# Two routed expert layers behind an attention: layer one's weights prepared in pieces of 1024 and 768 columns instead of 512 and 384

## The chip, the core and the metric

The kernel is written in Bass with the Tile framework and runs on one NeuronCore of one Trainium2 chip. The metric is device time in microseconds; a lower number is better. Five engines work side by side, each through its own instructions in a fixed order: TensorE (PE, with the weight load PEld), VectorE (DVE), ScalarE (ACT), GpSimd (POOL) and SyncE (SP). SP issues most of the transfers, POOL those that gather and scatter rows.

## The reference, cut to what matters

The input x has 7168 tokens of 192 numbers. An attention over the seven last tokens comes first, then a routed layer with eight experts and two experts per token, then a second one with one expert per token. The weights of a layer are the same size: per expert 192x1024 and 1024x192.

```python
x = attn_out.reshape(B * S, D)                       # weighted sum over the 7 last tokens
# layer one
noisy = x @ w_gate + np.log1p(np.exp(x @ w_noise)) * noise
top2 = np.argpartition(-noisy, 2, axis=1)[:, :2]     # two experts of eight
h = np.maximum(x[mask] @ w1[e], 0.0)
out[mask] += top2_w[mask, k, None] * (h @ w2[e])
# layer two
logits = xn @ en.T / tau                             # normalised rows
expert_idx = np.argmax(logits, axis=1)
h = np.maximum(x[mask] @ w1[e], 0.0)
out[mask] = gate_w[mask, None] * (h @ w2[e])
```

## The kernel before

**Tiles.** The 7168 tokens stand as 56 columns of 128. Layer one handles them in three groups of columns, 0 to 24, 24 to 40 and 40 to 56. For a group the attention is computed in chunks of four columns, each chunk's rows are written to a table in DRAM (`t`, line 490) and its router products go to `lg`. When all chunks of a group are there, `ctl` chooses the experts (line 511 on ACT is the first step of that, line 514 the first on DVE), ranks the entries (577 to 593), lays out slots (605 on), makes lists of row numbers by products of one-hots (767 to 770 on DVE, 760 on PE), and decodes them into `gx` (795). From then on 256-row tiles of one expert can run: POOL gathers rows (978), PE transposes them (1006), ACT copies them (1008), `first_product` (1028, with 1030 on ACT and 1031 on DVE) and `second_product` (1054, 1059) run by turns for neighbouring tiles, and POOL scatters the results (1062).

**Head and body.** The head runs until the first group's lists are decoded. It holds the attention of 24 columns (six chunks of seven products on DVE, line 385, summed by PE, line 412), their rows, the routing, and the preparation of layer one's weights. The body is the tiles of both layers with everything else beside them.

**Preparation.** The products run in 16-bit floats, so `prep_gen` scales each weight matrix by a power of two, cuts it into a high and a low half and writes both into a table in DRAM (`ws`). It takes two experts at a time and has two jobs for each pair, m = 0 for w1 (three `wo` tiles of 2048 columns out) and m = 1 for w2 (two of 3072). A job loads 32-bit weights into a stage (line 276 to 281; for layer one the stages are the two weight buffers `wb` and the end of `xh`), squares them on ACT for the sums (294), adds over partitions on PE (305 to 309), makes the scale `wsc` on DVE (311, 238 to 240), and then splits piece by piece: ACT writes the high half as scaled copy (334), DVE subtracts it from the scaled weight for the low half (336). A finished `wo` tile (there are three buffers) goes out on SP (340 to 346). The pieces are 512 columns of w1 and two rows of 192, that is 384, of w2. Before a tile can run, SP loads its expert's weights from `ws` into `wb` (line 996), which needs all writes of `ws`.

**What sets the order.** In the head, `prep_gen` is a chain that takes one step at every point, a step ending at each `yield`. Every job has a rank, a priority that counts up with its instructions; routing starts from 0, attention and preparation both from 2000, the loads of group two from 18000. The scheduler of the framework then orders each engine's instructions by readiness in its own model and by that priority. So fewer instructions in a job also move what stands around them. Each engine carries out its instructions strictly in the order that comes out. SP issues loads in order too, and a step that waits (line 490 waits for a chunk's rows) holds up everything behind it.

Of the kernel before, what the change touches and what calls it, by code (L numbers as in the profile page):

```python
# [39 lines left out]
class Layer:  # L40
    """Static plan of one routed layer: k entries per token, column groups of tokens."""

    def __init__(self, k, groups, mixed):
        self.k, self.groups = k, groups
        self.np = N * k // 256
        self.cap = [b * 128 * k // 256 for _, b in groups]
        self.sec = [0] + [cdiv(b * 128 * k - E * 255, 256) for _, b in groups[:-1]]
        # mixed: the slot by which the entries of all groups but the last have been run
        self.done = [(groups[-2][1] * 128 * k + E * 255) // 256] if mixed else []
        # Each run of slots is taken from its start and from its middle by turns, one weight buffer for either,  # L50
        # so that a buffer is loaded anew only where its own half passes on to another expert.
        cuts = self.sec + self.done + [self.np]
        self.buf, self.fresh, order = {}, [], []
        for a, b in zip(cuts, cuts[1:]):
            m = a + cdiv(b - a, 2)
            self.fresh += [a, m]
            u = 0
            for j in range(b - a):
                s = (a, m)[j % 2] + j // 2
                self.buf[s] = len(self.buf) % 2  # L60
                order.append(("p", s))
                # the single units follow the first pairs that hold entries of every group
                left = NS - j
                if a == self.sec[-1] and 0 < left <= NS:
                    order.append(("s", u))
                    u += 1
        assert len(order) == self.np + NS
        self.order = order
        self.pos = {o: i for i, o in enumerate(order)}
        self.first = [self.pos[("p", s)] for s in self.sec]  # L70
        self.units = 2 * self.np + NS
# [3 lines left out]
def two_moe(ctx: ExitStack, tc: tile.TileContext, x, wgen, w_gate, w_noise, noise, w1a, w2a, emb, tau, w1b, w2b, out):  # L75
# [12 lines left out]
    work = ctx.enter_context(tc.tile_pool(name="work", bufs=2))  # L88
    psum = ctx.enter_context(tc.tile_pool(name="psum", bufs=1, space=bass.MemoryType.PSUM))
    V, A, PE, SP, PL = nc.vector, nc.scalar, nc.tensor, nc.sync, nc.gpsimd  # L90
# [59 lines left out]
    # masks by partition: all, below 64, from 64 on  # L150
# [9 lines left out]
    # an entry's value: (1 + partition / 128) 2^(place - 56)  # L160
# [94 lines left out]
    @contextmanager  # L255
    def urgent(l):
        """work of a patient job that would wait for ever on an engine that is never idle."""
        low = tc.cur_priority
        if l:
            tc.cur_priority = state["here"]  # L260
        yield
        if l:
            state["here"] = tc.cur_priority
            tc.cur_priority = low

    def prep_gen(l, w1, w2):
# [21 lines left out]
        for i, (e, m) in enumerate(jobs):  # L288
# [32 lines left out]
            for c in range(3 if m == 0 else 2):  # L321
                wo = prep.tile([128, 3072], F16, name="wo", bufs=3)
                if m == 0:
                    n = 2048
                    w = 512
                    pieces = [(wo[:, f:f + w], wo[:, 1024 + f:1024 + f + w], st[:, 1024 * c + f:1024 * c + f + w]) for f in range(0, 1024, w)]
                else:
                    n = 3072
                    wv = wo.rearrange("p (g a d) -> p g a d", a=2, d=D)
                    sv = st[:, 1536 * c:1536 * c + 1536].rearrange("p (g d) -> p g d", d=D)  # L330
                    w = 2
                    pieces = [(wv[:, g:g + w, 0], wv[:, g:g + w, 1], sv[:, g:g + w]) for g in range(0, 8, w)]
# [40 lines left out]
    def after_tile():  # L373
        """work beside a tile that stays behind the tile's own work that was issued before."""
        return tc.issue_after(state["pin"].ins) if "pin" in state else ExitStack()

    def after_product():
        """TensorE's work beside the tiles, which stays behind the products that were issued before."""
        return tc.issue_after(state["pe"].ins) if "pe" in state else ExitStack()
# [116 lines left out]
    def top1(v, m, dst, n):  # L496
        """dst: one-hot of the first largest of v; m: the largest."""
# [130 lines left out]
    def add_phase(l, lo, hi, at=None):  # L628
        """the pairs lo .. hi of every expert get the slots from `at` on, or those behind the phase before."""
# [24 lines left out]
    def slot_experts(l, s0, s1):  # L654
        """the experts of pair slots s0..s1 (float)."""
        yield from threshold(l, iof[:, s0:s1], s1 - s0, exec_e[l][:, s0:s1])
# [20 lines left out]
    def exec_tables(l, a, b):  # L677
        """integer tables of the slots a..b: the expert, and whether the weights have to be loaded."""
# [25 lines left out]
    def rows_of(dst, r, t, sh, phases, l, n):  # L704
        """rows of the ranks r of every expert, in the given phases."""
# [21 lines left out]
    def list_gen(l, L, g, row, n, nu, u0):  # L727
        """the entries of group g by row: onehots of a row's unit and place, multiplied."""
# [57 lines left out]
    def decode(l, v, n, us):  # L786
        """v: integers as floats, 128 (place + 71) + partition, or 0."""
# [20 lines left out]
    def left_over(l, L, g, lrow, fb, u0, nu):  # L808
        """adds the units that the section before g kept: full pairs in their place, and the rest, at the rows lrow."""
# [20 lines left out]
    def section_open(l, L, g, key):  # L830
        """full pairs of the tokens so far run; the rest of each expert is kept behind the last slot."""
# [48 lines left out]
    def left_ranks(l, g):  # L880
        """the ranks at which the two units begin that section g keeps of every expert."""
# [6 lines left out]
    def section_last(l, L, key):  # L888
# [11 lines left out]
        if L.done:  # L900
            # the pairs that end the entries of the groups before stand first
# [64 lines left out]
    def run_by(b):  # L966
        """the tile of layer one by which all entries of the tokens below column b have been run."""
        return L1.pos[("p", L1.done[0])] if b <= G1[-2][1] else base2
# [14 lines left out]
    def slot(i):  # L983
        """a tile's place in the tables of its layer, and the weights it uses."""
# [3 lines left out]
    def weights(i, part):  # L988
        """part 0: the first product's weights, part 1: the second's."""
# [23 lines left out]
    def first_product(i, bg):  # L1013
        """in four parts, taken by turns with those of the second product of the tile before."""
# [137 lines left out]
    class Job:  # L1152
        """A generator of work with its key, the tile it may start after, and its place in the order of issue."""
# [15 lines left out]
    class Queue:  # L1169
        """Work beside the tiles: chains go one step a point, threads as far as their share of VectorE goes."""  # L1170
# [164 lines left out]
```

## Time and profile before

| | |
|---|---|
| time, median of 3 runs | 1094.52 us (1091.99 to 1097.86) |
| span of the profiled execution | 1096.0 us (no time of its own beside the span is given; it lies inside the range of the runs) |
| PE busy | 946.8 us, 86% of the span |
| DVE busy | 700.7 us, 64% |
| ACT busy | 605.3 us, 55% |
| POOL busy | 407.3 us, 37% |
| gx of the first group written | 137.2 us from the start |
| first product of the first tile | 148.7 us from the start |

The span is the time from the first to the last instruction of one execution. Busy shares are averages over stages with different limits: PE is busy nearly all the time after 150 us and hardly at all between 87 and 148 us, where DVE and ACT work. So the head has to be read by its own rows, in order of time, and the body by PE's waits. A row of the timeline gives the start, the duration, the engine, the line and the tiles, and in brackets how long the engine was idle before and what ended that.

### The profile page before, as it was taken

The numbers are of one execution on the slowest core, as the hardware profiler recorded it, in microseconds if no ns is written. First come the engines' busy times: TensorE is split into PE (matmuls) and PEld (weight loads), VectorE is DVE, ScalarE is ACT, GpSimd is POOL, SyncE is SP. The second block draws the span as 40 slices with busy tenths as digits, with TensorE's granted clock in tenths as the row PEclk, the third lists the DMA queues.
The fourth block names the chain that finished last, engine by engine and source line by source line (L and its number), as shares of the span: only waits on it lengthen the run. The fifth ranks groups of instructions, "written<-read, shape, count | busy, mean of one in ns | idle before, by whom it ended". The sixth has DMA issues, their size and how long they took to land.

```text
span 1096.0 us, 27746 instructions
## 1 busy us (share of the span) xinstructions
PE 946.8 (86%) x10250; PEld 853.9 (78%) x10250; DVE 700.7 (64%) x1943; ACT 605.3 (55%) x1337; POOL 407.3 (37%) x384
## 2 busy tenths in 40 slices
PE   5891259899989999998989998988788999999996
PEld 2551248788878888998979897877678899999896
DVE  8996969889688979553434433988676733333331
ACT  2999336666465765555555543975265344444442
POOL 1000054443445454344334443333344444445422
PEclk9996569999999999999899999999899999999999
DMA  8789674556568564779798977866675736888751
GB/s 269 216 271 293 224 249 143 149 190 200 158 207 285 167 208 142 260 215 329 263 367 292 333 270 229 264 216 180 205 252 160 256 125 217 288 300 306 260 190 41
DMA packets 99464, 251.81 MB, mean 230 GB/s; under 512 B 14207, under 2 KB 65119, under 8 KB 89856
## 3 DMA queue, kind: packets, MB, share of 16 engines
q1 hardware_dynamic: 81664, 215.03, 57.9%
q0 software_dynamic: 17664, 35.01, 11.5%
q8 instruction: 80, 1.31, 0.5%
q14 instruction: 56, 0.46, 0.1%
HBM read 246.09 MB, written 58.69 MB: 278 GB/s over the span
## 4 chain that ended last, share of the span: by engine, by line
PE 32%; DMA 5%; issue 5%; DVE 3%; ACT 3%; POOL 3%; SPq 1%; another core or an unknown queue 1%; POOLq 0%; ACTq 0%
PE ph L1028 15%; PE py L1054 14%; DMA wb<-ws 3%; DMA xh<-ws 2%; PE pt L1006 1%; POOL xg L978 1%; PE bt L468 1%; POOL yb L1062 1%; ACT hh L1030 1%; POOL ss L536 1%; SPq L281 1%; ACT xt L473 1%; ACT xh L448 1%; PE bl L479 1%
## 5 line engine op out<-in xcount | busy, mean ns | idle before, releaser
L1028 PE MATMUL ph<-xt,wb 128*128 128x256 f16 x3360 | 422.6, 276 | 10.0 <-DVE hl L1031 4.1
L1054 PE MATMUL py<-wb,hh 128*128 128x192 f16 x2688 | 361.9, 248 | 17.9 <-ACT ys L1059 13.4
L1030 ACT ACTIVATE hh<-ph 128x512 f16<-128x512 f32 (+1 forms) x400 | 221.4, 560 | 269.7 <-PE ph L1028 209.7
L1028 PEld LDWEIGHTS <-wb 128*128 128x128 f16 x3360 | 327.3, 99 | 47.9 <-issue 9.7
L978 POOL DMA_INDIRECT xg<-t,gx x184 | 196.3, 1067 | 376.0 <-PE pt L1006 157.9
L1054 PEld LDWEIGHTS <-hh 128*128 128x128 f16 x2944 | 266.6, 99 | 28.0 <-issue 18.7
L1031 DVE SCALAR_TENSOR_TENSOR wt<-ph,hh 128x512 f16<-128x512 f32 x200 | 137.4, 689 | 116.6 <-ACT hh L1030 95.2
L1062 POOL DMA_INDIRECT yb<-ys,sx x120 | 131.5, 1096 | 198.0 <-ACT ys L1059 173.9
L1054 PE MATMUL py<-wb,wt 128*128 128x192 f16 x800 | 198.3, 248 | 0.2 <-issue 0.2
L1031 DVE SCALAR_TENSOR_TENSOR hl<-ph,hh 128x512 f16<-128x512 f32 (+1 forms) x200 | 118.9, 603 | 111.2 <-ACT hh L1030 87.6
L1054 PE MATMUL py<-wb,hl 128*128 128x192 f16 x544 | 134.9, 248 | 0.1
L1059 ACT ACTIVATE ys<-py,sc 128x192 f32<-128x192 f32 x184 | 68.0, 415 | 90.1 <-PE py L1054 74.3
L1062 POOL DMA_INDIRECT out_dram<-ys,sx x64 | 64.5, 1007 | 95.6 <-ACT ys L1059 83.5
L385 DVE TENSOR_TENSOR tmp<-xh,wt 128x768 f32<-128x768 f32 x90 | 84.9, 954 | 0.8 <-PE ph L412 0.7
L1054 PEld LDWEIGHTS <-wt 128*128 128x128 f16 x800 | 78.9, 99 | 0.8 <-issue 0.6
L1008 ACT ACTIVATE xt<-pt 128x768 f16<-128x768 f16 x84 | 67.7, 807 | 7.0 <-PE pt L1006 6.9
L1039 DVE TENSOR_SCALAR sc<-xg,csl 128x2 f32<-128x2 f32 (+1 forms) x100 | 23.0, 231 | 75.8 <-ACT ys L1059 60.2
L1054 PEld LDWEIGHTS <-hl 128*128 128x128 f16 x672 | 66.6, 99 | 0.2
L473 ACT ACTIVATE xt<-bt 128x768 f16<-128x768 f16 x56 | 45.2, 807 | 31.8 <-PE bt L468 21.9
L1006 PE MATMUL pt<-identh,xg 128*128 128x128 f16 x552 | 48.7, 222 | 11.6 <-DMA xg<-t,gx 11.4
L1028 PE MATMUL ph<-xt,xh 128*128 128x128 f16 x640 | 45.9, 223 | 7.4 <-DMA xh<-ws 4.7
L1006 PEld LDWEIGHTS <-xg 128*128 128x128 f16 x552 | 39.1, 99 | 14.4 <-DMA xg<-t,gx 11.9
(302 smaller groups left out, 1079.0 us busy)
## 6 DMA issues: line engine op xcount, KB each, us to landing
wb<-ws SPq DMA_DIRECT2D x84, 1024.0 KB
wb<-ws SPq DMA_DIRECT2D x84, 768.0 KB
xh<-ws SPq DMA_DIRECT2D x16, 1024.0 KB
ws<-wo SPq DMA_DIRECT2D x16, 768.0 KB
xh<-ws SPq DMA_DIRECT2D x16, 768.0 KB
tmp<-yb SPq DMA_DIRECT2D x28, 384.0 KB
ws<-wo SPq DMA_DIRECT2D x16, 512.0 KB
ws<-wo SPq DMA_DIRECT2D x32, 256.0 KB
```

Of the source, the lines that this page charges most:

```text
L385: V.tensor_mul(dst.rearrange("p t (h g) -> p (t h) g", g=G), xv, w)
L473: A.activation(xt.rearrange("p a n -> p (a n)"), pa[:, 0:768], AF.Copy)
L978: PL.indirect_dma_start(out=xg[:, h], out_offset=None, in_=T[l][0:rows_in], in_offset=bass.IndirectOffsetOnAxis(ap=gidx[l][:, u + h:u + h ...
L1006: PE.transpose(pt[:, j, h], xg[:, h, 128 * b:128 * b + 128], identh)
L1008: A.activation(xt.rearrange("p j h n -> p (j h n)"), pt.rearrange("p j h n -> p (j h n)"), AF.Copy)
L1028: state["pe"] = mark = PE.matmul(ph[:, q, :n], s, m, start=j == 0, stop=j == 4)
L1030: A.activation(hh[:, fs, :n], ph[:, :, :n], AF.Relu)
L1031: state["pin"] = V.scalar_tensor_tensor(hl[:, fs, :n], ph[:, :, :n], 0.0, hh[:, fs, :n], op0=ALU.max, op1=ALU.subtract)
L1039: V.tensor_scalar(sc[:, :nh], xg[:, :nh, 192:193].bitcast(F32).rearrange("p h o -> p (h o)"), csl[l][:, c:c + 1], None, op0=ALU.mult)
L1054: state["pe"] = PE.matmul(py[:, h], t[:, f, hs], w2[:, f, c], start=f == 0 and j == 0, stop=f == 7 and j == 2)
L1059: A.activation(ys[:, h], py[:, h], AF.Copy, scale=sc[:, h:h + 1])
L1062: d = PL.indirect_dma_start(out=dst, out_offset=bass.IndirectOffsetOnAxis(ap=sidx[l][:, u + h:u + h + 1], axis=0), in_=ys[:, h], in_offset ...
```

## The change

In `prep_gen` the width of a piece depends on the layer. For layer one (l = 0) a piece of w1 has 1024 columns instead of 512 and one of w2 four rows of 192 (768) instead of two (384). Layer two keeps its pieces. The remaining lines of the diff take out comments.

```diff
@@ -322,13 +322,13 @@
                 wo = prep.tile([128, 3072], F16, name="wo", bufs=3)
                 if m == 0:
                     n = 2048
-                    w = 512
+                    w = 512 if l else 1024
                     pieces = [...]
                 else:
                     n = 3072
                     wv = wo.rearrange("p (g a d) -> p g a d", a=2, d=D)
                     sv = st[:, 1536 * c:1536 * c + 1536].rearrange("p (g d) -> p g d", d=D)
-                    w = 2
+                    w = 2 if l else 4
                     pieces = [...]
                 for h, lo, v in pieces:
                     A.activation(h, v, AF.Copy, scale=sc[:, c:c + 1])
                     yield 0.1
                     V.scalar_tensor_tensor(lo, v, sc[:, c:c + 1], h, op0=ALU.mult, op1=ALU.subtract)
                     yield 0.6
```

Layer one has four pairs of experts, and a pair had 6 pieces of w1 and 8 of w2. So 56 pieces, each one ACT and one DVE instruction, become 28. The order on the engines changes with it at three places.

ACT in the middle of the head, at the fourth chunk of the attention (its router row sums are line 430, its scaling 437, its copy 439). Before:

```order
L430 ACTIVATE rows,nrm<-ph 128x192 x4
L294 ACTIVATE junk,wnr<-wb_131 128x1024
L437 ACTIVATE xs<-ph,sx 128x192 x4
L334 ACTIVATE wo<-wb_130,wsc 128x2x192
L439 ACTIVATE rows<-xs 128x4x192
```

and now:

```order
L430 ACTIVATE rows,nrm<-ph 128x192 x4
L334 ACTIVATE wo<-wb_131,wsc 128x1024
L437 ACTIVATE xs<-ph,sx 128x192 x4
L294 ACTIVATE junk,wnr<-xh 128x768
L439 ACTIVATE rows<-xs 128x4x192
```

The preparation is one job further on: a split piece (334), which needs its job's scale `wsc`, stands where a square (294) stood, ahead of the chunk's scaling.

ACT at the end of the head, from the last chunk's scaling to the first step of the choice of experts (511). Before:

```order
L437 ACTIVATE xs<-ph,sx 128x192 x4
L334 ACTIVATE wo<-wb_131,wsc 128x512
L439 ACTIVATE rows<-xs 128x4x192
L334 ACTIVATE wo<-wb_131,wsc 128x512
L294 ACTIVATE junk,wnr<-xh 128x768
L294 ACTIVATE junk,wnr<-wb_130 128x1024
L473 ACTIVATE xt<-bt 128x768
L294 ACTIVATE junk,wnr<-wb_130 128x1024
L473 ACTIVATE xt<-bt 128x768
L294 ACTIVATE junk,wnr<-wb_130 128x1024
L511 ACTIVATE row<-lg 128x192
```

and now:

```order
L437 ACTIVATE xs<-ph,sx 128x192 x4
L439 ACTIVATE rows<-xs 128x4x192
L334 ACTIVATE wo<-wb_130,wsc 128x1024
L473 ACTIVATE xt<-bt 128x768
L294 ACTIVATE junk,wnr<-wb_131 128x768
L473 ACTIVATE xt<-bt 128x768
L294 ACTIVATE junk,wnr<-wb_131 128x768
L511 ACTIVATE row<-lg 128x192
```

Here too the preparation is one job further on when the choice begins: 34 of the 56 old pieces stood ahead of line 511, now 22 of the 28 new ones, and two of the last job's squares.

DVE in the lists of the first group (one-hots `ol`, `ou`, `orr`; PE multiplies them at line 760 into a `ph` bank). Before:

```order
L767 TENSOR_TENSOR ol<-jtab,rlf 128x1024
L770 TENSOR_TENSOR orr<-ou,vtab 128x512
L336 SCALAR_TENSOR_TENSOR wo<-wb_130,wsc,wo 128x512
L769 TENSOR_TENSOR ou<-jtab,rhf 128x512
L767 TENSOR_TENSOR ol<-jtab,rlf 128x1024
L770 TENSOR_TENSOR orr<-ou,vtab 128x512
L336 SCALAR_TENSOR_TENSOR wo<-wb_130,wsc,wo 128x512
```

and now:

```order
L767 TENSOR_TENSOR ol<-jtab,rlf 128x1024
L770 TENSOR_TENSOR orr<-ou,vtab 128x512
L769 TENSOR_TENSOR ou<-jtab,rhf 128x512
L770 TENSOR_TENSOR orr<-ou,vtab 128x512
L767 TENSOR_TENSOR ol<-jtab,rlf 128x1024
L769 TENSOR_TENSOR ou<-jtab,rhf 128x512
L767 TENSOR_TENSOR ol<-jtab,rlf 128x1024
```

No piece of the preparation is left between them, and two `orr` are made before the next `ol`. On SP the last writes of `ws` (340) now stand ahead of the load of group two's `xh` (117), which stood before them, and the loads of `wb` (996) follow that load.

## Rows read from the trace of the kernel before

**Rows 1.** Busy time by stretch: us, then PE, PEld, DVE, ACT, POOL busy (xcount), PEclk, DMA share, GB/s.
```profile
80.00:100.00 20.00, 7.00 (x76) 4.83 (x76) 11.35 (x36) 19.74 (x44) 0.00 (x0) 0.73 0.92 306
100.00:120.00 20.00, 0.38 (x3) 0.16 (x3) 19.29 (x78) 15.43 (x30) 0.00 (x0) 0.50 0.73 240
140.00:160.00 20.00, 11.55 (x80) 8.57 (x81) 10.15 (x16) 6.04 (x10) 11.38 (x11) 0.64 0.79 277
```

**Rows 2.** Timeline, pieces in a row: start, us, engine, line, tiles, forms, count.
```profile
34.25 3.40 DVE L336 SCALAR_TENSOR_TENSOR wo<-wb,wsc,wo 128x512 f16<-128x512 f32 x5
45.84 1.68 DVE L336 SCALAR_TENSOR_TENSOR wo<-wb,wsc,wo 128x384 f16<-128x384 f32 x3
59.97 3.17 ACT L334 ACTIVATE wo<-xh,wsc 128x512 f16<-128x512 f32 x5
40.10 2.13 ACT L334 ACTIVATE wo<-wb,wsc 128x384 f16<-128x384 f32 x4 [0.26 <-DVE wsc L239]
47.83 1.05 ACT L294 ACTIVATE junk<-xh 128x1024 f16<-128x1024 f32 x1
48.78 0.20 ACT L294 ACTIVATION_READ_ACCUMULATOR junk<-xh 128x1 f32 x1
```

**Rows 3.** Timeline of ACT and DVE, the steps of the first group's routing.
```profile
98.38 0.35 ACT L511 ACTIVATE row<-lg 128x192 f32<-128x192 f32 x1
100.43 0.36 DVE L514 TENSOR_TENSOR row<-row,nz 128x192 f32<-128x192 f32 x1 [1.01 <-ACT row L512]
112.21 0.17 DVE L605 TENSOR_SCALAR shr_t<-cnt 128x8 int32<-128x8 f32 x1
120.56 0.69 DVE L767 TENSOR_TENSOR ol<-jtab,rlf 128x1024 bf16<-128x1024 bf16 x1
134.65 0.23 DVE L780 TENSOR_SCALAR dv<-ph 128x64 int32<-128x64 int32 x1 [0.68 <-PE ph L760]
137.21 0.20 DVE L795 TENSOR_TENSOR gx<-dfv,df 128x34 int32<-128x34 f32 x1
```

**Rows 4.** Timeline of ACT and SP: last chunk's row sums, and a load with its reader.
```profile
87.60 0.32 ACT L430 ACTIVATE rows<-ph 128x192 f16<-128x192 f32 x1
46.44 1.44 SPq L281 DMA_DIRECT2D wb<-in_moe_w_dram  x2
55.60 0.84 ACT L294 ACTIVATE junk<-wb 128x768 f16<-128x768 f32 x1 [0.42 <-DMA wb<-in_moe_w_dram]
```

**Rows 5.** Timeline of PE and DVE inside the lists.
```profile
125.03 1.13 PE L760 MATMUL ph<-orr,ol 128*128 128x64 bf16 x8 [1.12 <-DVE orr L770]
127.28 1.13 PE L760 MATMUL ph<-orr,ol 128*128 128x64 bf16 x8 [1.12 <-DVE orr L770]
126.20 0.69 DVE L767 TENSOR_TENSOR ol<-jtab,rlf 128x1024 bf16<-128x1024 bf16 x1 [0.22 <-PE ph L760]
```

**Rows 6.** Timeline of POOL, SP, PE and ACT, from the gather to the first product.
```profile
137.71 1.14 POOL L978 DMA_INDIRECT xg<-t,gx  x1 [133.78 <-DVE gx L795]
139.16 1.21 POOL L978 DMA_INDIRECT xg<-t,gx  x1 [0.30 <-issue]
140.15 0.36 SPq L996 DMA_DIRECT2D wb<-ws  x1
141.99 0.50 PE L1006 MATMUL pt<-identh,xg 128*128 128x128 f16 x3 [7.37 <-DMA xg<-t,gx]
146.50 0.50 PE L1006 MATMUL pt<-identh,xg 128*128 128x128 f16 x3 [4.01 <-DMA xg<-t,gx]
147.04 0.81 ACT L1008 ACTIVATE xt<-pt 128x768 f16<-128x768 f16 x1 [6.53 <-PE pt L1006]
148.69 3.57 PE L1028 MATMUL ph<-xt,wb 128*128 128x256 f16 x16 [1.68 <-DMA wb<-ws]
```

**Rows 7.** Timeline of DVE and POOL, the second group's lists in the body.
```profile
292.53 0.19 DVE L795 TENSOR_TENSOR gx<-dfv,df 128x32 int32<-128x32 f32 x1
297.71 0.69 DVE L1031 SCALAR_TENSOR_TENSOR hl<-ph,hh 128x512 f16<-128x512 f32 x1 [1.85 <-issue]
293.49 1.00 POOL L978 DMA_INDIRECT xg<-t,gx  x1 [9.46 <-PE ph L1028]
```

**Rows 8.** PE's waits from 148 us on: us in total, times, longest us.
```profile
PE py L1054 <- ACT ys L1059: 13.4, 7, 4.5
PE ph L1028 <- DMA wb<-ws: 3.5, 3, 1.7
```

## The prediction

> **What bounds the kernel now.** I read the busy time by stretch first, then the timeline of the head engine by engine, then PE's waits in the body. From 150 us on PE is nearly always busy, and what it waits for there is small: 13.4 us on the output copies of tiles, 3.5 us on weights [rows 8]. So the change, which touches only layer one's preparation, can act in two ways: by the moment at which the first product starts (148.69 us, [rows 6]), and by the order that the body inherits.
>
> The head has three parts. Until about 81 us DVE is full with the attention's products. From 80 to 100 us ACT is the limit: 19.74 of 20 us busy, while DVE is at 11.35 [rows 1]. Then comes the routing of the first group, from line 511 on ACT at 98.38 us to `gx` at 137.21 us, a chain through DVE, which is busy 19.29 of the 20 us from 100 on [rows 1, 3]. After `gx` comes the gather, and the first product starts 11.5 us after `gx` [rows 3, 6]. The preparation's pieces lie in all three parts, since 22 of its 56 old pieces are still to come at line 511. On DVE they stand between the routing's steps.
>
> **The change part by part.**
>
> *Price of a piece.* Five DVE pieces of 512 take 3.40 us and the last alone 0.75, so the step from one to the next is 0.66 us; three of 384 take 1.68, a step of 0.53 [rows 2]. The slope is 1.0 ns a column, so 1024 columns should step by 1.20 and 768 by 0.93: 0.13 us saved for each pair that becomes one, 28 x 0.13 = 3.6 us on DVE. On ACT the steps are 0.61 (512) and 0.505 (384), and a copy-like activation of 1024 columns, the square, starts its next row 0.95 us later [rows 2]. Interpolated, 768 is 0.75 to 0.78. So a pair saves 0.27 us there, 28 x 0.27 = 7.5 us. If none of it is hidden and all of it counts, the head gains these 3.6 to 7.5 us, which is less than 0.7%. What decides is where the pieces lie now.
>
> *Up to line 511.* ACT now does 22 new pieces instead of 34 old ones before line 511. That is 10 x 0.95 + 12 x 0.75 = 18.5 us instead of 18 x 0.61 + 16 x 0.505 = 19.1 us, and in addition two squares of the last job at 0.9: ACT's own work before line 511 grows by 1.2 us although each column is cheaper. To this come waits, because the preparation stands ahead of the attention's small steps. I walked through the new order of ACT and DVE with the steps above and with all other instructions at their durations in the trace. The largest gap is at the fourth chunk: ACT's row sums end at about 70 us, and the piece behind them needs a scale that DVE, after its row of attention products, makes only at about 74.5 us. ACT idles 4.4 us and the chunk's scaling waits behind it. Before, a square without such a need stood there. The last chunk's row sums come at about 96.6 us in this walk instead of 87.60 [rows 4], and line 511 at 105.6 instead of 98.38: **+7.2 us**. Between the bounds of +1.2 (only the work) and +9.0 (the lag of the last chunk's row sums in full) I take the walk.
>
> *From line 511 to gx.* Four sections, each from [rows 3]. Line 514 to 605 is 11.8 us with eight pieces of 384 and two of 512 in it (5.6 us); now there are two of 1024 and three of 768 (5.2 us), but the sums of the last job stand in the choice on DVE (line 311). Their second load is issued on SP only after the last chunk's rows, near 102 us; a pair of loads and the reader of its second one were 9.2 us apart [rows 4], so the sums are ready near 111 us and the choice waits some 1.4 us: +1.0. Line 605 to 767: 8.35 us, one piece less and small steps gone, but dependent steps then stand bare: -0.45. The lists, 767 to 780, take 14.1 us now. The loop is PE's eight products (1.13 us), then `ol`, then `orr`, then PE again, 2.25 us a block, since `orr` stands behind an `ol` that waits for PE [rows 5]. In the new order two `orr` come first, PE runs two blocks back to back, and the pair takes 3.38 instead of 4.5 us: 11.1 us for the six blocks, -3.0. Line 780 to `gx`: 2.56 us, with three pieces of 384 out of it, -1.3. Sum **-3.75 us**, so `gx` comes at 137.2 + 7.2 - 3.75 = 140.7 us.
>
> *From gx to the first product.* The first half of the gather lands 3.1 us after its issue ends, the second 6.1 us, because the loads of `wb` start at 140.15 us in between; and the first product then waits for `wb`, about 0.75 us after the copy on ACT would allow it [rows 6]. In the new order the last piece is out some 20 us before `gx`, so the writes of `ws` and the loads of `wb` come before the gather. The relief is 3.0 + 0.75 = **-3.75 us**; its bounds are that and 0, since the 1.5 MB load of `xh` now stands right before the loads of `wb`, and 5 MB at the 240 to 306 GB/s of these stretches [rows 1] last 17 to 22 us from about 121 us on, to about 140 us.
>
> Together the first product starts at 148.69 + 7.2 - 3.75 - 3.75 = **148.4 us, 0.3 us earlier**.
>
> *The body.* Same instructions, but DVE's order puts the second group's `gx` three `hl` steps (line 1031) later against the tiles than before; these end at 298.4 instead of `gx` at 292.53 [rows 7], so up to 5.7 us later. POOL waits for this `gx` with a gather three tiles ahead (9.46 us idle, [rows 7]) and PE shows no wait for these rows; what can reach PE is only scatters that are held up behind it, by way of the output copies [rows 8]. Bounds 0 and +5.7; near the first, since the gather is early: **+1.5 us**.
>
> *Weighing a rule.* The rows show a saving of 0.13 us on DVE and 0.27 us on ACT a merged pair [rows 2]. The Trainium skill, Perfetto Trace Analysis, section "Optimizing Scalar/DVE Operations", gives about 60 ns on DVE and 93 ns on ScalarE of busy time for each instruction, and says that larger operations help if the engine is saturated; by an estimate from that page the 28 pairs would save 1.7 us on DVE and 2.6 us on ACT. The rows' larger savings are used here. The same section says that where these engines are not saturated but cause bubbles on others, breaking instructions up may finish work sooner; the head from 80 us on, where DVE is at 57%, is such a place, and the rule speaks against the change there.
>
> **The sum.** 1094.5 (median; the profiled span of 1096.0 is 1.5 us above it, within the runs) - 0.3 + 1.5 = **1095.7 us**. No change that a measurement tells: 0.5% (5.5 us) is about what it can.
>
> **The rivals.**
>
> *The chain is not late (faster).* If the waits in the walk don't come about, line 511 is later by the 1.2 us of work alone. Then `gx` is at 134.7 us and the first product starts 6.3 us earlier; with no delay in the body that is 1088.2 us. For it speaks that DVE and ACT both have less to do; against it the 4.4 us gap, which is a matter of order alone.
>
> *The gather stays crowded (slower).* If line 511 is 9.0 us late and the loads of `wb`, held up behind the 1.5 MB of `xh`, are still under way when the gather starts, the relief is lost: 9.0 - 3.75 + 1.5 = +6.75 us, 1101.3 us. It decides from the point at which the last `wb` load lands after `gx`. For it speaks the 140 us worked out above, against it that the first tile's own weights are first in the row.
>
> *The pieces don't get cheaper by merging.* If a 768 piece with its rows of 192 costs what two of 384 do, the order still moves. Then 16 pairs cost 0.27 us more on ACT and 0.13 more on DVE than reckoned above; most of it lies before line 511, so +3 us: 1098.7 us. Nothing in the trace speaks for it, as the steps rise in proportion from 384 to 512.
>
> **How the numbers follow.** My forecast gets 0.55, the faster rival 0.20, the slower one 0.20, the dear pieces 0.05. The forecast's own bounds, from a lag at line 511 of some 3 us less to the full lag, and 0 to 5.7 us in the body, are 1091 to 1102. The range takes in the middle of the faster rival and the slower rival's time: 1088 to 1103 us. Faster by over 0.5% (below 1089.0) gets 0.19, within 0.5% 0.58, slower (above 1100.0) 0.23.
>
> **What would show it.** In the profile of the changed kernel: DVE pieces of 1.2 and 0.93 us and ACT pieces of 0.95 and 0.75 us a step; an ACT wait for `wsc` of some 4 us near 70 us; line 511 at 105 us; lists of 11 us without pieces between them; `gx` near 140.7; the two halves of the first gather about 1.5 us apart at PE; the first product near 148.4 us; and the same sum of PE's waits after it. The prediction is wrong if line 511 stays below 100 us, if the second half of the gather still comes 4 us behind the first, or if PE waits over 5 us more in the body than before.

## The result and the profile after

| | before | after |
|---|---|---|
| time, median of 8 runs each | 1094.88 us (1091.99 to 1097.86) | 1099.97 us (1098.93 to 1107.29) |
| span of the profiled execution | 1096.0 us | 1101.8 us (its own time 1103.94 us) |
| line 437 of the first chunk (ACT) | 29.67 us | 37.52 us |
| row sums of the last chunk (430, ACT) | 87.60 us | 101.42 us |
| line 511 (ACT) | 98.38 us | 111.36 us |
| gx of the first group (795, DVE) | 137.21 us | 145.49 us |
| first load of `wb` (996, SP) | 140.15 us | 133.13 us |
| first product (1028, PE) | 148.69 us | 151.79 us |

The ratio after to before is 1.0056, with a 95% interval of 1.0038 to 1.0075: 5.1 us more in the medians. The interval lies above 1, so the kernel is slower; the time is inside the range that was given. The profiled execution of after is 4.0 us above its own median; so I take times of the head from it and not the total.

The head has to be read first. This is ACT at the first chunk before the change (timeline: start, duration, engine, line, tiles; in brackets the idle time before and what ended it):

```profile
28.22 0.84 ACT L294 ACTIVATE junk<-wb 128x768 f16<-128x768 f32 x1
29.67 0.73 ACT L437 ACTIVATE xs<-py,sx 128x192 f32<-128x192 f32 x2 [0.51 <-DVE sx L239]
...
37.80 0.79 ACT L473 ACTIVATE xt<-bt 128x768 f16<-128x768 f16 x1
38.49 0.32 ACT L430 ACTIVATE rows<-ph 128x192 f16<-128x192 f32 x1
```

and after it, from the same square on (`...` stands for rows left out, here and below):

```profile
27.74 0.84 ACT L294 ACTIVATE junk<-wb 128x768 f16<-128x768 f32 x1
...
29.05 3.23 ACT L334 ACTIVATE wo<-wb,wsc 128x1024 f16<-128x1024 f32 x3 [0.37 <-DVE wsc L239]
32.18 0.83 ACT L294 ACTIVATE junk<-wb 128x768 f16<-128x768 f32 x1
...
37.52 0.71 ACT L437 ACTIVATE xs<-py,sx 128x192 f32<-128x192 f32 x2
...
44.48 0.81 ACT L473 ACTIVATE xt<-bt 128x768 f16<-128x768 f16 x1 [1.61 <-PE bt L468]
46.42 0.81 ACT L473 ACTIVATE xt<-bt 128x768 f16<-128x768 f16 x1 [1.12 <-PE bt L468]
47.12 0.32 ACT L430 ACTIVATE rows<-ph 128x192 f16<-128x192 f32 x1
```

Three pieces (3.1 us) and five squares more (32.18 to 37.52, 5.3 us) stand ahead of the first chunk's scaling. ACT carries them out back to back and the scaling starts 7.85 us later. That chunk's transposes on PE and their copies (473) follow it, and the next chunk's row sums stand behind those copies on ACT: they come at 47.12 instead of 38.49 us. In the two gaps of 1.61 and 1.12 us ACT waits for PE.

What a wide piece costs is read from these rows of after and from the pieces of 1024 on ACT above and below (several in a row against one alone gives the step from one to the next):

```profile
31.23 3.67 DVE L336 SCALAR_TENSOR_TENSOR wo<-wb,wsc,wo 128x1024 f16<-128x1024 f32 x3
38.73 0.95 ACT L334 ACTIVATE wo<-wb,wsc 128x768 f16<-128x768 f32 x1
40.29 2.59 ACT L334 ACTIVATE wo<-wb,wsc 128x768 f16<-128x768 f32 x3
43.09 3.80 DVE L336 SCALAR_TENSOR_TENSOR wo<-wb,wsc,wo 128x768 f16<-128x768 f32 x4
50.09 1.28 DVE L336 SCALAR_TENSOR_TENSOR wo<-xh,wsc,wo 128x1024 f16<-128x1024 f32 x1
```

The second place is the fourth chunk, ACT and then DVE after the change:

```profile
70.92 0.81 ACT L473 ACTIVATE xt<-bt 128x768 f16<-128x768 f16 x1 [2.07 <-PE bt L468]
...
79.55 1.15 ACT L334 ACTIVATE wo<-wb,wsc 128x1024 f16<-128x1024 f32 x1 [4.22 <-DVE wsc L239]
80.60 1.34 ACT L437 ACTIVATE xs<-ph,sx 128x192 f32<-128x192 f32 x4
```

```profile
75.22 1.82 DVE L385 TENSOR_TENSOR tmp<-xh,wt 128x768 f32<-128x768 f32 x2
76.96 0.16 DVE L311 TENSOR_REDUCE wss<-st 128x2 f32<-128x4 f32 x1
77.03 0.95 DVE L385 TENSOR_TENSOR tmp<-xh,wt 128x768 f32<-128x768 f32 x1
...
79.34 0.17 DVE L239 TENSOR_SCALAR wsc<-q 128x3 int32<-128x3 int32 x1
```

The piece on ACT stands ahead of the chunk's scaling and waits 4.22 us for `wsc`, whose steps on DVE stand between products of the attention. The chunk's scaling waits with it.

From line 511 on, the rows that answer to [rows 3, 6]:

```profile
111.36 0.36 ACT L511 ACTIVATE row<-lg 128x192 f32<-128x192 f32 x1
113.44 0.36 DVE L514 TENSOR_TENSOR row<-row,nz 128x192 f32<-128x192 f32 x1 [2.10 <-ACT row L512]
125.53 0.16 DVE L605 TENSOR_SCALAR shr_t<-cnt 128x8 int32<-128x8 f32 x1
133.53 0.69 DVE L767 TENSOR_TENSOR ol<-jtab,rlf 128x1024 bf16<-128x1024 bf16 x1
144.13 0.23 DVE L780 TENSOR_SCALAR dv<-ph 128x64 int32<-128x64 int32 x1 [1.27 <-PE ph L760]
145.49 0.20 DVE L795 TENSOR_TENSOR gx<-dfv,df 128x34 int32<-128x34 f32 x1
```

```profile
133.13 5.93 SPq L996 DMA_DIRECT2D wb<-ws  x4
145.98 1.14 POOL L978 DMA_INDIRECT xg<-t,gx  x1 [142.05 <-DVE gx L795]
148.85 0.50 PE L1006 MATMUL pt<-identh,xg 128*128 128x128 f16 x3 [4.76 <-DMA xg<-t,gx]
150.39 0.50 PE L1006 MATMUL pt<-identh,xg 128*128 128x128 f16 x3 [1.04 <-DMA xg<-t,gx]
151.79 4.70 PE L1028 MATMUL ph<-xt,wb 128*128 128x256 f16 x30 [0.90 <-ACT xt L1008]
```

Line 511 is 13.0 us later. The way from there to `gx` takes 34.1 instead of 38.8 us, mostly since no piece stands in the lists any more (10.6 instead of 14.1 us). From `gx` to the first product it takes 6.3 instead of 11.5 us: the loads of `wb` started 12 us before `gx`, the halves of the gather come 1.5 us apart, and nothing waits for weights. So 3.1 of the 13 us are left at the first product.

Three of PE's waits in the body (from 148 us on; us in total, times, longest) are

```profile
PE bl L479 <- ACT xt L473: 13.1, 10, 6.2
PE py L1054 <- ACT ys L1059: 11.3, 8, 4.1
PE ph L1028 <- DMA wb<-ws: 10.0, 3, 7.4
```

against 12.0 us for `bl` before and [rows 8] for the other two: 2.1 us less on output copies, 6.5 more on weights. The second group's `gx` comes later too:

```profile
303.24 0.19 DVE L795 TENSOR_TENSOR gx<-dfv,df 128x32 int32<-128x32 f32 x1
```

10.7 us behind [rows 7], 7.6 of it beyond the first product's own lag. All of PE's waits that the view lists from each kernel's first product on add up to 70.1 us before and 73.9 us after.

### The profile page after: what moved, and what is told of

Same layout as the page of the kernel before. It is cut to its first block, busy times and chain, and to the rows that moved or that the text cites. A ratio compares the mean times of both kernels' runs of the same rounds, so it can differ in the third digit from the quotient of the medians.

```text
span 1101.8 us, 27673 instructions
## 1 busy us (share of the span) xinstructions
PE 949.1 (86%) x10250; PEld 855.1 (78%) x10250; DVE 700.7 (64%) x1915; ACT 603.1 (55%) x1309; POOL 408.7 (37%) x384
## 3 DMA queue, kind: packets, MB, share of 16 engines
q0 software_dynamic: 17664, 35.01, 10.7%
## 4 chain that ended last, share of the span: by engine, by line
PE 52%; DVE 17%; ACT 9%; issue 8%; DMA 8%; POOL 3%; SPq 2%; another core or an unknown queue 1%; POOLq 0%; DVEq 0%; ACTq 0%
PE ph L1028 23%; PE py L1054 20%; DMA wb<-ws 4%; DVE tmp L385 3%; DVE acc L400 2%; PE pt L1006 2%; DVE hl L1031 2%; PE bt L468 2%; ACT hh L1030 1%; DVE wt L1031 1%; POOL xg L978 1%; ACT xt L473 1%; DVE wo L336 1%; PE py L412 1%
## 5 line engine op out<-in xcount | busy, mean ns | idle before, releaser
L1028 PEld LDWEIGHTS <-wb 128*128 128x128 f16 x3360 | 326.9, 99 | 55.8 <-DMA wb<-ws 10.7
L1062 POOL DMA_INDIRECT yb<-ys,sx x120 | 134.5, 1121 | 210.2 <-ACT ys L1059 186.6
L1028 PEld LDWEIGHTS <-xh 128*128 128x128 f16 x640 | 40.6, 100 | 10.3 <-DMA xh<-ws 6.5
```

Of the source, the lines that this page charges most:

```text
L1028: state["pe"] = mark = PE.matmul(ph[:, q, :n], s, m, start=j == 0, stop=j == 4)
L1062: d = PL.indirect_dma_start(out=dst, out_offset=bass.IndirectOffsetOnAxis(ap=sidx[l][:, u + h:u + h + 1], axis=0), in_=ys[:, h], in_offset ...
```

## The experiments

The question is whether the wide pieces lose the time themselves or the order that comes with them. The scheduler does not look at widths alone: at every point the preparation makes one step, and a piece ends two of them. With half as many pieces the preparation needs half as many points, and so is one job ahead of the attention. The steps can be given back without touching the pieces. All of these kernels ran on chips on which the kernel before takes 1070 to 1071 us instead of 1094.9; ratios are to runs of before on the same chip, all with their 95% interval. Times inside the kernel are from one profiled execution each.

**e1: wide pieces, old order.** Two steps and two priorities more for each wide piece:

```diff
-                    V.scalar_tensor_tensor(lo, v, sc[:, c:c + 1], h, op0=ALU.mult, op1=ALU.subtract)
-                    yield 0.6
+                    V.scalar_tensor_tensor(lo, v, sc[:, c:c + 1], h, op0=ALU.mult, op1=ALU.subtract); yield 0.6
+                    for d in () if l else (0.1, 0.6): tc.cur_priority += 1; yield d
```

> Layer one's pieces stay at 1024 and 768 columns, but each is given the two steps and the two places in the priority that its second half had, so the preparation stands among the attention's steps as it did before the change (17 of 28 pieces ahead of line 511, four, one and five in the sections behind it). Theory 'order': the scaling of the first chunk (line 437) is back near 30 us, line 511 comes at or ahead of the old 98.4 us, at 95 to 98, since 17 pairs save some 0.18 us each on ACT; the first product at 145 to 148.5; time 1089 to 1094, 0.995 to 0.999 of before. Rival 'wide pieces': a piece of 1.0 to 1.3 us holds up the small steps behind it wherever it stands; line 511 stays above 105 us and the time near 1100, 1.005 of before.

Measured: 1069.96 us, ratio 0.9991 (0.9971 to 1.0011). The scaling is back at 30.16 us, line 511 at 98.67, the first product at 149.01. The loss is gone with the order; but line 511 and the first product come a little later than the expectation's 95 to 98 and 145 to 148.5 us, and the gain that was expected from cheaper pieces isn't clear of noise. Its rows on ACT say where it went:

```profile
77.92 0.73 ACT L437 ACTIVATE xs<-py,sx 128x192 f32<-128x192 f32 x2 [2.04 <-DVE sx L239]
87.37 0.33 ACT L430 ACTIVATE rows<-ph 128x192 f16<-128x192 f32 x1 [0.79 <-DMA t<-rows]
98.67 0.36 ACT L511 ACTIVATE row<-lg 128x192 f32<-128x192 f32 x1 [0.79 <-DVE lg L483]
100.14 0.93 ACT L334 ACTIVATE wo<-xh,wsc 128x768 f16<-128x768 f32 x1 [1.11 <-DMA ws<-wo]
```

The fifth chunk's row sums come 2.5 us earlier than before (74.53 against 77.06), the last chunk's only 0.2 (87.37 against 87.60). Between 80 and 100 us ACT is busy for 16.8 us instead of 19.74 [rows 1], and waits for DVE and for transfers in its place.

**e2: old pieces, new order.** Only every second old piece ends a step:

```diff
-                for h, lo, v in pieces:
+                for k, (h, lo, v) in enumerate(pieces):
                     A.activation(h, v, AF.Copy, scale=sc[:, c:c + 1])
-                    yield 0.1
+                    yield 0.1 if l or k % 2 else 0.0
                     V.scalar_tensor_tensor(lo, v, sc[:, c:c + 1], h, op0=ALU.mult, op1=ALU.subtract)
-                    yield 0.6
+                    yield 0.6 if l or k % 2 else 0.0
```

> The old pieces of 512 and 384 columns, but of each pair only the second ends a step, so the preparation stands one job further on, as in the changed kernel (44 of 56 pieces ahead of line 511, eleven, one and none in the sections behind). Theory 'order': late like the changed kernel and a little more, since the pieces are dearer: line 511 at 111 to 116 us, time 1100 to 1106, 1.005 to 1.011 of before. Rival 'wide pieces': with narrow pieces nothing is late; line 511 at 98 to 101 us, time 1093 to 1096, 0.998 to 1.002.

Measured: 1079.16 us, ratio 1.0084 (1.0062 to 1.0106); line 511 at 115.29, the first product at 156.62 us. The narrow pieces lose time in the new order as well, and more than the wide ones. So it is the order that loses it. The price of the pieces can be estimated here: the changed kernel (e6, below) is at 1.0050, which puts merging 28 pairs at 0.34%, 3.6 us, in the new order. The two ratios come from two chips, and their intervals together leave 0.06 to 0.62%. In the old order e1 against before has 0.09%, and its interval includes zero. So how much time the cheaper pieces save by themselves is not well known.

**e3 and e4: one size alone.** `w = 512 if l else 1024` with `w = 2`, and `w = 512` with `w = 2 if l else 4`.

> Only w1's pieces are widened (1024), w2's stay at 384: 12 of the 28 merged pairs. Theory 'order': at the first chunk its order is that of the full change (three pieces and ten squares ahead of line 437, before: none and five), so line 437 there is near 37 us and line 511 at 105 to 111; time 1096 to 1101, 1.002 to 1.006 of before. Rival 'wide pieces': the loss goes by the share of the pieces, 12 of 28 of 5 us: 1097, 1.002; both sizes together, this run and the next, add up to the whole loss.

> Only w2's pieces are widened (768), w1's stay at 512: 16 of the 28 merged pairs. Theory 'order': the first chunk stands as before (no piece and five squares ahead of line 437), later chunks between before and after; line 511 at 98 to 104 us, time 1092 to 1097, 0.998 to 1.003 of before. Rival 'wide pieces': 16 of 28 of 5 us, 1098, 1.003.

Measured: e3 1073.28 us, 1.0031 (1.0012 to 1.0050), scaling of the first chunk at 38.02, line 511 at 107.26, first product at 153.62 us. e4 1066.98 us, 0.9967 (0.9945 to 0.9989), scaling at 29.51, line 511 at 99.57, first product at 146.47 us: better than the 0.998 to 1.003 that was expected. The rival wanted the two to add up to the whole loss, and they don't (-0.02% against +0.5%): the three wide pieces of the very first job make the first chunk late, and e4 leaves that job alone.

**e5 and e6: both kernels again, side by side.**

> The kernel before once more, for a trace from the same chip as the next three. The four runs e1 to e4 have between 917.9 and 920.3 us from the first product to the end, wherever the first product starts (146.5 to 156.6 us). Theory 'the start decides': the kernel before has the same 917 to 921 us on such a chip and its first product at 148 to 149.5. Rival 'the body's order costs as much as the start': its rest is 2 us or more shorter than that of the changed kernel beside it.

> The changed kernel once more, beside the kernel before on this chip. Theory 'the start decides': first product at 151 to 153 us, 3 us behind that of before, and the time longer by 3 to 4 us, 1.003 to 1.004. Rival 'the body's order': the loss is 1.0055 again, and the 2 to 3 us beyond the first product's lag are in the body, the second group's gx some 10 us later than before.

Measured: before 1069.84 us in one run (median of 29 others 1071.09), first product at 147.78. After 1075.35 us, ratio 1.0050 (1.0033 to 1.0067), first product at 151.04. So of 4.3 us in the medians 3.3 are there at the first product and 1.0 comes behind it; the second group's `gx` is 8.4 us later. The ratio was 1.003 to 1.004 in the first theory and 1.0055 in the second; the interval takes in both and doesn't part them.

**e7 and e8: one job's steps given back.** The line of e1 with `if l or not (i == 0)` and `if l or not (i == 3)`.

> The changed kernel, but only the pieces of the first job (three of w1, the job whose squares and pieces stand ahead of the first chunk's scaling) get the two steps and two priorities of their second halves back; the other 25 pieces are as in the changed kernel. By its order the first chunk's scaling has no piece and five squares ahead of it, as before. Theory 'the first chunk's scaling': line 437 of that chunk near 30 us instead of 37.5, the chunks' row sums up to 74.5 as in e1, line 511 at 97 to 102 us, the first product at 146 to 150; 0.996 to 1.001 of before. Rival 'the lag is made piece by piece along the head': one job of seven in the head is too little, line 511 above 106, 1.004.

> The same for the fourth job alone (its pieces are those that wait for the scale near 75 us): the first chunk's scaling stays late, the pieces at the fourth and fifth chunk stand further back. Theory 'the first chunk's scaling is 8 to 9 of the 13 us, the wait for the scale the other 4': row sums of the second and third chunk as late as in the changed kernel (47 and 60 us), the ACT wait for wsc near 75 us gone or under 1.5 us, line 511 at 106 to 109 us; time 1.000 to 1.005 of before. Rival 'piece by piece': line 511 about 109 to 111, 1.005.

Measured: e7 1071.46 us, 0.9996 (0.9979 to 1.0013), scaling at 28.85, line 511 at 99.33. Three pieces' steps take 11.4 us off line 511 against e6 (110.69), since the order behind the first chunk comes back with them; so e7 does not measure the first chunk by itself. e8 1066.28 us, 0.9971 (0.9949 to 0.9994), scaling late at 38.52, line 511 at 106.12: 4.6 us less than e6. The wait at the fourth chunk is gone; e6 first, then e8:

```profile
78.50 1.15 ACT L334 ACTIVATE wo<-wb,wsc 128x1024 f16<-128x1024 f32 x1 [4.47 <-DVE wsc L239]
76.04 1.36 ACT L437 ACTIVATE xs<-ph,sx 128x192 f32<-128x192 f32 x4 [2.16 <-DVE sx L239]
```

The piece that waited 4.47 us for `wsc` in e6 no longer stands ahead of that scaling, which waits 2.16 us for its own `sx`. That piece has 1024 columns and is the first of the fifth job, not one of the fourth's, as the expectation had it; what e8 gives back to the fourth job puts the fifth behind the scaling. With e3, which has the late first chunk without the long wait for `wsc` (line 511 at 107.26), this puts some 8 to 9 us of the 12 on the first chunk and 3 to 5 on the wait. It is an estimate, since each of the two also moves what stands behind the place that it changes.

The time of e8 missed its expectation (1.000 to 1.005): line 511 is 7.7 us later than in before, the first product at the same time, and the kernel is 0.29% faster. So its gain lies behind the first product.

e7 and e8 show something else besides. By `gx` e7 is 5.3 us ahead of e8, and by the first product 0.7:

```profile
136.29 18.55 SPq L996 DMA_DIRECT2D wb<-ws  x5
136.65 1.14 POOL L978 DMA_INDIRECT xg<-t,gx  x1 [132.72 <-DVE gx L795]
144.51 0.50 PE L1006 MATMUL pt<-identh,xg 128*128 128x128 f16 x3 [9.75 <-DMA xg<-t,gx]
147.14 6.14 PE L1028 MATMUL ph<-xt,wb 128*128 128x256 f16 x30 [0.90 <-ACT xt L1008]
```

```profile
133.43 21.66 SPq L996 DMA_DIRECT2D wb<-ws  x5
141.92 1.14 POOL L978 DMA_INDIRECT xg<-t,gx  x1 [137.99 <-DMA wb<-ws]
146.05 0.89 PE L1006 MATMUL pt<-identh,xg 128*128 128x128 f16 x6 [6.01 <-DMA xg<-t,gx]
147.83 5.70 PE L1028 MATMUL ph<-xt,wb 128*128 128x256 f16 x30 [0.90 <-ACT xt L1008]
```

The first block is e7 (SP, POOL, PE), the second e8. Where the loads of `wb` start at about the time of the gather, the gather takes 7.9 us from its issue to PE; where they are 8 us ahead, 4.1 us. Over the kernels so far, `gx` to the first product is 6.3 or 6.4 us where the loads are 8 us or more ahead of `gx`, and 10 to 11 us everywhere else. Another difference runs along with this one: in before, e1, e3, e4 and e7 a 0.5 MB load of layer two's weights (line 276) stands 1 to 3 us ahead of the loads of `wb`, and in after, e2 and e8 none does. So which of the two holds up the gather is not shown.

| | line 511 | gx | loads of wb | first product | gx to product | time less first product |
|---|---|---|---|---|---|---|
| before (e5) | 98.46 | 137.31 | 140.25 | 147.78 | 10.5 | 923.3 |
| after (e6) | 110.69 | 144.79 | 132.42 | 151.04 | 6.3 | 924.3 |
| e1 | 98.67 | 138.30 | 138.44 | 149.01 | 10.7 | 921.0 |
| e2 | 115.29 | 150.28 | 136.33 | 156.62 | 6.3 | 922.5 |
| e3 | 107.26 | 143.44 | 141.30 | 153.62 | 10.2 | 919.7 |
| e4 | 99.57 | 136.48 | 137.45 | 146.47 | 10.0 | 920.5 |
| e7 | 99.33 | 136.15 | 136.29 | 147.14 | 11.0 | 924.3 |
| e8 | 106.12 | 141.43 | 133.43 | 147.83 | 6.4 | 918.5 |

Two chains meet ahead of the first product: attention, routing and gather, and the last pieces, the writes of `ws` and the loads of `wb`. In all of these traces but that of before the first product waits last for the copy of the gathered rows (0.90 us for `xt`, line 1008), and not for weights; so where the second chain sets the time, it must do so through the gather.

The last column is the median time less the first product of the profiled execution (for before, the median of 1071.09). It varies by 6 us, and no single wait of PE goes with it. In the profiled executions the span less the first product is 923.8 us in e6 and 925.1 in e7, and 917.9 to 920.3 in the other six. There PE's own busy time goes with it: from the first product on it is 864.5 and 864.4 us in e6 and e7 and 858.7 to 861.7 in the others, for the same products. The first pair of traces doesn't show this (869.5 us before, 868.0 after), and no run was made to find its reason.

**e9 to e11: the load of `xh` moved behind the first loads of `wb`.** In e7, e4 and before:

```diff
     load_w(*G1[1])
-    load_x(*G1[1])
...
             weights(i, part)
+    with tc.issue_after(loads[1].ins): load_x(*G1[1])
```

> As e7 (first job's steps kept), and SP's 1.5 MB load of the second group's xh stands behind the first two loads of wb instead of ahead of the last four writes of ws. In e7 gx came at 136.15 us but the first half of the gather only 8.4 us later, since the loads of wb had started at 136.29; in the changed kernel they started at 133.13 and the gather was fast. Theory 'two chains meet': the second chain, last pieces, writes of ws, loads of wb, ends at 145 to 147 us in e7 and hides what the routing gained; without 1.5 MB ahead of it (some 5 us at 280 GB/s) the loads of wb start at 131 to 135, the first product at 142 to 145, 0.993 to 0.997 of before. Rival 'the writes wait for the pieces, not for the transfers': the loads of wb start at 135 to 136.5 as in e7, the first product at 146 to 148, and the second group's attention is later, 0.999 to 1.003.

> As e4 (only w2 in wide pieces), with the load of xh moved behind in the same way. Theory 'two chains meet': first product at 142 to 145 instead of 146.5, 0.993 to 0.996. Rival: first product at 146 to 147, 0.996 to 1.000.

> The kernel before with the load of xh moved behind in the same way, pieces untouched. Theory 'two chains meet': the loads of wb start some 3 us earlier than 140.15 us, first product 144 to 147 instead of 147.8, 0.996 to 0.999. Rival: 140 again, 147 to 149, 0.999 to 1.003.

Measured: e9 1070.85 us, 1.0003 (0.9986 to 1.0019), loads of `wb` at 137.67, first product at 146.81. e10 1066.44 us, 0.9965 (0.9951 to 0.9979), 135.49 and 146.22. e11 1070.39 us, 1.0000 (0.9989 to 1.0011), 140.21 and 146.20. In e9 and e11 the loads start no earlier without the 1.5 MB ahead of them, and in e10 the 2.0 us gained at them are 0.25 at the first product. For the loads and the time the rival holds: the writes wait for the last pieces. In e9 (DVE, then SP):

```profile
130.15 1.01 DVE L336 SCALAR_TENSOR_TENSOR wo<-wb,wsc,wo 128x768 f16<-128x768 f32 x1
132.39 1.01 DVE L336 SCALAR_TENSOR_TENSOR wo<-wb,wsc,wo 128x768 f16<-128x768 f32 x1
```

```profile
128.93 4.84 SPq L340 DMA_DIRECT2D ws<-wo  x2
137.67 5.94 SPq L996 DMA_DIRECT2D wb<-ws  x4
```

The last pieces stand in the lists, 2.2 us apart; the last write is out at 133.8 us, and the loads come 3.9 us later. The first product of e11, 146.20 us, is 1.6 us earlier than in before; that lies in the theory's range and not in the rival's 147 to 149, though the loads don't move and the time doesn't either. Its gather shows why the loads of `wb` can't be all that makes a half late (SP, then PE):

```profile
140.21 5.97 SPq L996 DMA_DIRECT2D wb<-ws  x4
142.36 0.50 PE L1006 MATMUL pt<-identh,xg 128*128 128x128 f16 x3 [8.02 <-DMA xg<-t,gx]
143.11 0.50 PE L1006 MATMUL pt<-identh,xg 128*128 128x128 f16 x3 [0.25 <-DMA xg<-t,gx]
```

They start when they started in before (140.25 in e5), between the issue of the second half and its landing, and this half is 0.75 us behind the first instead of 3.5 (e5) and 4.5 [rows 6]. The 0.5 MB load of line 276 that starts at 139.28 us in e5, right beside the second half's issue, starts at 121.8 us in e11, where two of 0.25 MB (line 278) start from 136.8 us on instead. Which transfers hold up the gather was not tried any further.

The best of these kernels are e4, e10 (both with wide pieces for w2 only) and e8; at 0.9967, 0.9965 and 0.9971 they can't be told from one another.

## Why the prediction was right or wrong

The time, 1099.97 us, was 4.3 us above the forecast of 1095.7 and within the range; that it came so near is in part luck, since errors of both signs met. The step that failed is the term up to line 511: +7.2 us in the sum, 13.0 in the trace (12.2 on the later chip), outside its bounds of 1.2 to 9.0. The others made up for part of it: 5.8 us more there, 1.0 less from line 511 to `gx`, 1.45 less from `gx` to the first product, and 0.5 more behind it give the 3.9 us by which the 5.1 measured exceed the 1.2 forecast.

- **Up to line 511.** The mechanism, the preparation standing ahead of the attention's small steps, was right. But the only place that the prediction names is the fourth chunk, and by the estimate from e3 and e8 the larger part, some 8 us, comes from the first chunk, of which it says nothing. The gap of ACT for `wsc`, 4.4 us in the walk, is 4.22 in the trace, though at 75 to 80 us and not near 70. The size was wrong, and the walk with it: it went through ACT and DVE and left out PE. It gave 96.6 us for the last chunk's row sums, measured 101.42. Up to there ACT waits three times for PE's transposes (`xt <- bt`): 1.61, 1.12 and 2.07 us, 4.8 together (4.7 in four waits in e6). The list of ACT's waits of before has none of them. The pieces that are dearer than reckoned (next point) add 9 x 0.09 + 11 x 0.07 = 1.6 us to that; as much must have come back elsewhere, and I can't show where. So the waits for PE fit the missing time by their size, and no run takes them away by themselves. From these row sums to line 511 another 0.9 us is missing in the walk (9.9 us instead of 9.0), where ACT waits for the same transposes for 1.0 and 0.4 us. The upper bound was made from the same walk, and so could not hold what the walk left out.
- **The price of a piece.** DVE as forecast: three of 1024 in 3.67 us and one alone 1.28, a step of 1.195, and 0.93 for 768. ACT was mis-sized: three in 3.23 and one alone 1.15 make a step of 1.04 instead of 0.95, and 768 steps by 0.82 instead of 0.75 to 0.78. The square's step had been read as the copy's, and only up to the square's own accumulator row at 48.78 us [rows 2], not to the next instruction. A pair saves 0.18 to 0.19 us on ACT, not 0.27. With these steps, and 0.97 for a square of 768, ACT's own work ahead of line 511 grows by 3.1 us and not by 1.2. The Trainium skill, Perfetto Trace Analysis, section "Optimizing Scalar/DVE Operations", has about 60 ns on DVE and 93 ns on ScalarE for an instruction on SBUF; the 0.13 and 0.18 us here are twice that. Its rule that smaller instructions may finish sooner where an engine isn't saturated but makes others wait spoke against the change. No run here shows such a gain: with the new order the smaller pieces (e2) have a ratio of 1.0084 against 1.0050, with the old order (before against e1) there is no difference clear of noise.
- **Line 511 to gx.** -4.7 us instead of -3.75. The lists are 10.6 us (forecast 11.1; three pairs at 3.38 instead of 4.5 us save 3.4 and not 3.0, which gives 10.7), 780 to `gx` 1.4 (forecast 1.3), 605 to 767 8.0 (forecast 7.9). The wait of the choice for the last job's sums did not come (+0.3 instead of +1.0); why was not looked into.
- **gx to the first product.** -5.2 us instead of -3.75, outside the bounds of -3.75 and 0: the relief was there in full and more, and the rival of the crowded gather fell. Part of the 11.5 us had been read as the second half alone; with the loads 12 us ahead the first half is faster too, 2.9 us from its issue to PE instead of 4.3 [rows 6]. That the second half was late because of the loads of `wb` is not shown; e11 has them at the same time and the half on time.
- **The body.** +1.5 us forecast; 2.0 from the medians (5.1 less 3.1), 1.0 in e6. Its cause stays open. The second group's `gx` is 7.6 us later beyond the first product's lag, above the bound of 5.7. The sum of PE's waits from the first product on rose by 3.8 us (70.1 to 73.9), under the 5 us that were named as a sign of being wrong, and in e5 and e6 it is the same (50.6 and 50.9). The weights' wait of 7.4 us in after (586 us) is not it: e4 and e8 have one of over 5 us at a like place (566 and 568 us) and are faster than before.
- **The rivals.** That the chain isn't late fell with line 511. That the pieces don't get cheaper fell with the steps: 768 columns take 0.82 us on ACT and 0.93 on DVE, two of 384 took 1.01 and 1.06. The slower rival had the late line 511 but the wrong reason, since its gather was not crowded. That it is the order and not the pieces is shown: e1 takes the loss away with the pieces wide, e2 makes it with the pieces narrow.

## What to carry to other kernels

Where a scheduler hands out work by steps, the size of an instruction is also its place in the queue: merge instructions, and look first at what now stands ahead of the small steps that others wait for; giving the merged piece its old number of steps takes that loss away. A walk through a new order has to hold every engine on the chain, above all the one that seems to have time. And before paying for an earlier chain, look for the second one that meets it: here 13 us on one were 3 us at the first product, and getting 11 of them back (e7) was worth less than 4 of the time.

## What was not expected of the hardware

The gather of 128 rows took 2.9 us from the start of its issue to PE when the loads of `wb` had started 12.9 us earlier (after: 145.98 to 148.85), and 7.9 us when they started 0.4 us before it (e7: 136.65 to 144.51). In the old kernel it was the second half that came late [rows 6]. Which of the transfers beside it does this is open: e11 has the loads of `wb` at the same time and the second half on time. The same kernel took 1094.9 us on one chip and 1070 to 1071 on others, with the first product at 148.69 and 147.78 us: nearly all of that difference is in the body, at a mean granted clock of 0.950 and 0.954. PE's waits from the first product on are 70.1 us in the one trace and 50.6 in the other (e5), which is most of it. Why was not looked into.
